# A four-part scheme for the first FFN layer extended to one more chunk of tokens, with attention visits, residual loads and operand splits moved earlier

## The chip, the cores and the metric

One core of one Trainium2 chip runs the whole kernel. The metric is the device time of one execution in microseconds (us); the time before is the median of three runs. Engines are called PE (TensorE; PEld its weight loads), DVE (VectorE), ACT (ScalarE), POOL (GpSimd) and SP (SyncE, which here issues most DMAs). Each engine runs its instructions in the order in which the code writes them.

## The reference

```
# attention, 8 batches x 8 heads, 576 tokens, head size 64
mask  = band of 32 (heads 0-3)  or  every 32nd earlier token (heads 4-7)
attn  = softmax(where(mask, q @ k.T / 8, -1e9)) @ v
x     = attn, heads side by side          # [8, 576, 512]
# layer norm and feed-forward
xn    = (x - mean(x)) / sqrt(var(x) + 1e-6) * g_ln
out   = x + relu(xn @ w_ch1) @ w_ch2      # w_ch1 [512, 2048], w_ch2 [2048, 512]
```

## The kernel before

**Tiles and chunks.** The 8 x 576 token rows are cut into nine chunks of 512: chunk c < 8 holds the first 512 tokens of batch c, chunk 8 the last 64 tokens of all batches. In the code `wide` is 7, `FIRST` is 3, A is chunk 7 and Z is chunk 8. The hidden size 2048 is 16 blocks f of 128. All matmuls of the feed-forward run on pairs of float32r tiles, a high part and a rest ("hi", "lo", made by `split_x`: ACT copies the high part, DVE or POOL subtracts), three matmuls for one product. The mean and the scale of the layer norm are folded into the weights and into a factor per row that is applied at the end (`x_scale` makes it from a load of x, `finish` applies it).

**Stages.** Chunk 0 is interleaved with the first attention by a word list (`ORDER`). Chunks 1 and 2 are `plain`: for each f, twelve matmuls of 512 columns of the first layer (`ffn1`), relu, and twelve of the second layer (`group`). Chunks 3 to 5 run `pair(c, p)` eight times, for two blocks f each: seven products of 128x256 blocks (`product2`, Strassen's scheme in Winograd's form: P1 a11 b11, P6 s2 t2, P5 s1 t1, P2 a12 b21, P7 s3 t3, P4 a22 t4, P3 s4 b22, in that order) in place of eight, sums on DVE (`add2`), and second-layer groups between the products. The operands b.. and t.. of x are staged in freed weight tiles (`stage_x`, `move`), sums t.. by POOL (`stage_sums`), then split (`x_split`). Sums of weights are made by POOL (`w_sums`), stored to DRAM (sd) and loaded again one pair ahead (`stage_w`, `split_w`). Chunk 6 is `plain` again. The joint part runs chunks 7 and 8 together in the same scheme with 512 columns, over operands `whole`/`halfs`, with weights that come back from DRAM through rings (`w_fetch`, `s_fetch`, `s_split`). Then the second layer of Z.

**Attention visits.** A batch has four head pairs. A visit does the scores of the next pair and the values of the present one on PE, then mask, division and maximum on DVE, subtraction on POOL, exp on ACT, a transpose on DVE, a store to DRAM and a load of the turned weights (pd, pt). In plain chunks the generator `pieces` hands out steps, four for each f; in `pair` a visit stands at every even p. Before the change, chunk c visits the four pairs of batch c + 1.

**Lines that the prediction touches.** L1214 `move` copies a weight half over one that `a_store` (L1243) has saved to DRAM (ad). L745/L747 load x for the residual and L752 (`x_scale`) reads it; in `half_c` the tables are

```
LOADS.update({2: (12, 13, 13, 14), **{u: (4, 5, 8, 9) for u in range(FIRST, wide - 1)}})
SCALES.update({2: (14, 15, 15, NFC), **{u: (7, 7, 11, 11) for u in range(FIRST, wide - 1)}})
```

L574 is the division of a visit, L1326 `add2`, L1148 `turn` (a DVE transpose of what `tail`, L773, loads for chunk 8), L721 and L802 the subtractions of splits, L867/L874 `ffn1`, L884 its rest part hl, L916 the second layer, L1321 `product2`, L1491 the joint products.

Of the kernel before, what the change touches and what calls it, by code (L numbers as in the profile page):

```python
# [63 lines left out]
def kernel(  # L64
# [10 lines left out]
    nc = tc.nc  # L75
# [257 lines left out]
    class Pair:  # L333
# [280 lines left out]
        def x_blocks(self, xT=None):  # L614

            cc = self.h0 // 2
            if xT is None and self.b == 2:
                xT = self.xo.rearrange("p t h d -> p (t h d)")[:, 0:CH]
            if xT is not None:
# [3 lines left out]
            elif self.b == B - 2:  # L623
                nc.vector.transpose(spread[cc], self.xraw.rearrange("p (i x) -> p i x", i=2))
            else:
                d, j = divmod(cc, 2)
                for i, name in enumerate((("b11", "t1"), ("b21", "b22"))[d]):
                    nc.vector.transpose(stage_x(name)[:, j], self.xraw[:, HC * i:HC * (i + 1)])
                if d == 0 and (self.b > 3 or j):
                    stage_sums(j)  # L630
# [174 lines left out]

# [27 lines left out]
    def whole_tile(i, names):  # L833
        t = wp.tile([P, 2, CH], F32, tag=f"w1_{i}", name=f"whole{i}_{names[0]}")
# [251 lines left out]
    def pieces(i0, i1):  # L1086
        for i in range(i0, i1):
            now = pairs[i] if i >= 2 * NHP else None
            nxt = pairs[i + 1] if i + 1 < NP else None
            short = i < 3 * NHP - 1 or i in (29, 30)  # L1090
            later = i in (3 * NHP, 3 * NHP + 1)
            soon = short and nxt and not nxt.local
            m_piece(now, nxt)
            yield
            if i + 2 < NP:
                pairs[i + 2].load_v()
# [3 lines left out]
            if now:  # L1100
                now.x_raw(nc.scalar)
            if nxt:
                nxt.p_turned()
            yield
            if nxt:
                nxt.v_sums()
# [22 lines left out]
            if later:  # L1129
                now.x_blocks()  # L1130
# [4 lines left out]
    gen = pieces(2 * NHP - 1, 4 * NHP)  # L1135
# [11 lines left out]
    def turn(cc):  # L1147
# [3 lines left out]
    last_steps = {  # L1151
        1: [lambda: tail(2)],
        3: [lambda: whole_tile(1, ("b220", "b120")), lambda: turn(2)],
        4: [lambda: tail(0)],
        5: [lambda: half_x(4, "b220")],
        6: [lambda: turn(0), lambda: whole_tile(2, ("t10", "t20")), lambda: whole_tile(3, ("t30", "t40")),
            lambda: sums_x(0, nc.gpsimd)],
        7: [lambda: half_x(5, "t10"), lambda: half_x(6, "t20"), lambda: tail(3)],
        8: [lambda: half_x(7, "t30")],
        9: [lambda: half_x(8, "t40"), lambda: whole_tile(1, ("b221", "b121")), lambda: turn(3)],  # L1160
        10: [lambda: half_x(9, "b221")],
        11: [lambda: tail(1), lambda: s_fetch(0)],
        12: [lambda: s_split(0)],
        13: [lambda: turn(1), lambda: whole_tile(2, ("t11", "t21")), lambda: whole_tile(3, ("t31", "t41")),
             lambda: sums_x(1, nc.vector)],
        14: [lambda: half_x(11, "t11"), lambda: half_x(12, "t21"), lambda: half_x(13, "t31"),
             lambda: half_x(14, "t41"), lambda: w_fetch(0)],
        15: [lambda: w_fetch(1), lambda: s_fetch(1)],
    }

    A_RING, S_RING = (0, NFC - 1, 1), (10, 2, 3)
# [435 lines left out]
```

## Time and profile before

| | |
|---|---|
| median of 3 runs | 923.51 us (922.21 to 923.74) |
| profiled execution | 921.0 us, span 919.2 us |
| granted TensorE clock, mean | 0.986 |
| PE busy | 875.8 us (95%), 7837 instructions |
| DVE busy | 534.9 us (58%) |
| POOL busy | 323.7 us (35%) |
| ACT busy | 264.7 us (29%) |
| DMA | 142.42 MB, mean 155 GB/s |

The busy time of an engine counts its instructions' time; PE's matmuls overlap each other, so the distance between the starts of two matmuls, not the duration of one, tells what a matmul costs. A row of the timeline has start, duration, engine, line, operation, tiles and shape, and in brackets the idle time before it and what ended that.

### The profile page before, as it was taken

To read this page: it belongs to the slowest core of one execution; us is meant where nothing else is said; L and a number is where in the kernel's file an instruction comes from. 1 tells how busy PE (TensorE), PEld (TensorE's weight loads), DVE (VectorE), ACT (ScalarE), POOL (GpSimd) and SP (SyncE) were. 2 spreads that over 40 slices of the span, in tenths; PEclk is the share of its full clock that TensorE was granted. 3 is DMA by queue.
4 is the path that set the end of the run, shared out by engine and by line. 5 is a ranking of instruction groups with operands and counts; after the bars stand their busy time and mean duration, and the time that the engine had idled before them with its cause. 6 is when DMAs were issued, how large, how long until landed. Compare 5 with 4: busy or idle time off the path is not lost.

```text
span 919.2 us, 20228 instructions
## 1 busy us (share of the span) xinstructions
PE 875.8 (95%) x7837; PEld 730.0 (79%) x7837; DVE 534.9 (58%) x1108; ACT 264.7 (29%) x531; POOL 323.7 (35%) x380
## 2 busy tenths in 40 slices
PE   7799999999989979999999989999988999999997
PEld 6688888888878868888888878887766888787886
DVE  5899974556524457666756676666355442333443
ACT  3786631111111132233333242322112122111121
POOL 5787750011237834435534462331012111121000
PEclk9999999999999999999999999999999999999999
DMA  9899865577469786979796969777663252331111
GB/s 188 196 287 249 254 122 112 125 158 145 88 173 205 197 191 163 216 182 195 179 199 160 225 146 217 166 213 159 152 114 94 48 184 92 116 102 46 41 52 47
DMA packets 381545, 142.42 MB, mean 155 GB/s; under 512 B 297605, under 2 KB 361993, under 8 KB 381449
## 3 DMA queue, kind: packets, MB, share of 16 engines
q1 hardware_dynamic: 298120, 126.24, 55.2%
q10 hardware_dynamic: 83328, 14.89, 9.4%
q8 instruction: 62, 1.02, 0.5%
q14 instruction: 35, 0.28, 0.1%
HBM read 100.37 MB, written 40.70 MB: 153 GB/s over the span
## 4 chain that ended last, share of the span: by engine, by line
PE 31%; DMA 9%; DVE 5%; SPq 3%; issue 1%; ACT 1%; ACTq 0%; POOL 0%; DVEq 0%; POOLq 0%
PE po L916 16%; PE x L1491 7%; PE x L1321 4%; DMA pd<-sm 2%; PE ph L867 1%; DMA v_l<-in_v_dram 1%; DMA pt<-pd 1%; SPq L773 1%; DMA x<-xds 1%; PE m L455 1%; DVE hz L1510 1%; DVE u L1326 1%; PE ph L874 1%; PE n L524 1%; DMA v_s<-in_v_dram 1%
## 5 line engine op out<-in xcount | busy, mean ns | idle before, releaser
L916 PE MATMUL po<-w,hh 128*128 128x512 f32 x768 | 241.2, 396 | 0.0
L916 PEld LDWEIGHTS po<-w,hh 128*128 128x128 f32 x768 | 143.3, 190 | 29.9 <-issue 0.4
L916 PE MATMUL po<-w,hq 128*128 128x512 f32 x576 | 160.2, 394 | 0.9 <-DVE x L890 0.7
L916 PE MATMUL po<-w,hl 128*128 128x512 f32 x384 | 150.6, 392 | 0.0
L916 PEld LDWEIGHTS po<-w,hq 128*128 128x128 f32 x576 | 97.4, 189 | 12.5 <-ACT w L1257 0.8
L884 DVE SCALAR_TENSOR_TENSOR hl<-ph,hh 128x512 fp32r<-128x512 f32 x64 | 43.8, 684 | 97.2 <-ACT hh L879 97.2
L501 POOL TENSOR_TENSOR sm<-sm,mx 128x640 f32<-128x640 f32 (+1 forms) x31 | 40.2, 1298 | 139.2 <-DVE mx L496 125.8
L1321 PE MATMUL x<-xh_b,w 128*128 128x256 f32 x384 | 84.3, 282 | 2.7 <-DVE p L1326 1.6
L916 PEld LDWEIGHTS po<-w,hl 128*128 128x128 f32 x384 | 72.7, 189 | 15.6
L879 ACT ACTIVATE hh<-ph 128x512 fp32r<-128x512 f32 x64 | 38.0, 593 | 145.0 <-PE ph L874 121.4
L867 PE MATMUL ph<-xh,w 128*128 128x512 f32 x188 | 75.2, 400 | 2.4 <-DVE hl L884 2.4
L867 PE MATMUL ph<-xl,w 128*128 128x512 f32 x188 | 74.0, 394 | 0.0
L1258 POOL TENSOR_TENSOR w<-sw,w 128x256 fp32r<-128x256 f32 x48 | 37.6, 804 | 102.9 <-ACT w L1257 81.6
L1321 PEld LDWEIGHTS x<-xh_b,w 128*128 128x128 f32 x384 | 65.4, 188 | 10.0 <-issue 3.0
L757 POOL TENSOR_TENSOR rs<-rs,mhalf 128x1 f32<-128x1 f32 x36 | 20.2, 562 | 146.6 <-DVE rs L756 146.5
L1321 PE MATMUL x<-xl_b,w 128*128 128x256 f32 x192 | 53.8, 280 | 0.0
L507 ACT ACTIVATE sm<-sm 128x648 f32<-128x648 f32 (+1 forms) x32 | 23.8, 744 | 98.5 <-POOL sm L501 98.5
L874 PE MATMUL ph<-xh,w 128*128 128x512 f32 x188 | 51.2, 395 | 0.0
L1192 POOL TENSOR_TENSOR rings<-stage,rings 128x512 fp32r<-128x512 f32 x16 | 20.6, 1290 | 79.9 <-ACT rings L1191 79.9
L867 PEld LDWEIGHTS ph<-xh,w 128*128 128x128 f32 x188 | 35.5, 189 | 10.1 <-DVE hl L884 2.8
L874 PEld LDWEIGHTS ph<-xh,w 128*128 128x128 f32 x188 | 35.7, 191 | 7.6
L867 PEld LDWEIGHTS ph<-xl,w 128*128 128x128 f32 x188 | 35.6, 189 | 7.1
(232 smaller groups left out, 1683.8 us busy)
## 6 DMA issues: line engine op xcount, KB each, us to landing
s<-in_moe_w_ch_dram SPq DMA_DIRECT2D x32, 512.0 KB
sw<-sd SPq DMA_DIRECT2D x48, 256.0 KB
out_dram<-x SPq DMA_DIRECT2D x32, 256.0 KB
raw<-in_q_dram SPq DMA_DIRECT2D x108, 72.0 KB
raw<-in_k_dram SPq DMA_DIRECT2D x108, 72.0 KB
wd<-w SPq DMA_DIRECT2D x24, 256.0 KB
ringa<-wd SPq DMA_DIRECT2D x24, 256.0 KB
xds<-xo SPq DMA_DIRECT2D x32, 162.0 KB
```

Source lines behind the costliest of these rows:

```text
L501: eng.tensor_tensor(out=sm, in0=sm, in1=mx[:, :, 0:nt].unsqueeze(3).broadcast_to([P, 2, nt, sm.shape[3]]), op=ALU.subtract)
L507: nc.scalar.activation(out=self.smv, in_=self.smv, func=AF.Exp, scale=SCALE)
L757: nc.gpsimd.tensor_tensor(out=rs, in0=rs, in1=mhalf, op=ALU.pow)
L867: nc.tensor.matmul(ph, w1h[:, cc], x[:, cc, :], start=(new and n == 0 and i == 0), stop=False)
L874: nc.tensor.matmul(ph, w1l[:, cc], xt[c][0][:, cc, :], start=False, stop=(cc == NCC - 1))
L879: nc.scalar.activation(out=hh, in_=ph, func=AF.Relu)
L884: nc.vector.scalar_tensor_tensor(out=hl, in0=ph, scalar=0.0, in1=hh.bitcast(F32), op0=ALU.max, op1=ALU.subtract)
L916: nc.tensor.matmul(po[c, i], hx, w, start=(n_po[c, i] == 0 and n == 0), stop=(n_po[c, i] == NFC - 1 and n == 2))
L1192: nc.gpsimd.tensor_tensor(out=t[:, :, 1], in0=stage[n], in1=t[:, :, 0].bitcast(F32), op=ALU.subtract)
L1258: nc.gpsimd.tensor_tensor(out=w[:, 1], in0=t[:, k], in1=w[:, 0].bitcast(F32), op=ALU.subtract)
L1321: nc.tensor.matmul(ps, wx, xx[:, j], start=(start and j == 0 and i == 0), stop=(j == 1 and i == 2), skip_group_check=not start)
L1491: nc.tensor.matmul(ps, wx, xx, start=(start and j == 0 and i == 0), stop=(j == 1 and i == 2), skip_group_check=not start)
```

## The change

Chunk 6 runs `pair` like chunks 3 to 5. Every visit stands one place earlier: chunk 1 and 2 do ten visits in place of nine, chunk c's visit at p = 0 is already the second pair of batch c + 1, and chunk 6 has three visits. The first pair of a batch is visited at p = 6 of the chunk before, its x comes back from DRAM at p = 1 and is staged at p = 3. In the last pair of chunks 3 to 5 each operand is split right behind the product that used it last (`X_AT`); in the last Strassen chunk a table (`final`) places the loads, turns, sums and splits for the joint part. The stores and reloads of saved weight halves (ad, `a_store`, `a_back`, `back`) go. Six of the eight `w_sums` move from chunk 2 to chunk 1. Residual loads of chunk 2 go to steps 4, 5, 7, 8 and the scales to 7, 8, 10, 11; in pairs there is one load for each of p = 2 to 5 and one scale at the end of p = 3 to 6. The joint part begins with pairs 7 and 6, whose weights are still in SBUF, has rings of 3 and 2 tiles where there were 3 and 3, one spare tile where there were two, and the product s1 t1 two places later.

```
-    SUMS_AT = 1, 2, 5, 6, 7, 9, 10, 11
-    plain(1, NT)
+    plain(1, {f: [partial(w_sums, p)] for p, f in enumerate((1, 2, 3, 9, 11, 13))}, NT)
...
+    plain(2, {
+        1: [partial(w_sums, 6)],
+        2: [partial(w_sums, 7)],
+        3: [pairs[3 * NHP].x_blocks],
+        7: [pairs[3 * NHP + 1].x_blocks],
+        11: [partial(stage_sums, 0)],
+        12: [partial(stage_sums, 1), partial(stage_w, 0)],
+        13: [partial(x_split, "b11")],
+        14: [partial(x_split, "t2"), partial(x_split, "t1"), partial(split_w, 0), partial(stage_w, 1)],
+        15: [partial(stage_w, 2)],
+    }, 1)
...
+    final = {
+        (1, "P1"): [lambda: whole_tile(1, ("b210", "b110"))],
+        (1, "P6"): [lambda: tail(2)],
+        (2, "P6"): [lambda: tail(0)],
+        (2, "P3"): [lambda: whole_tile(5, ("b220", "b120")), lambda: turn(2)],
+        (3, "P1"): [lambda: whole_tile(0, ("b211", "b111"))],
+        (3, "P5"): [lambda: turn(0)],
+        (3, "P2"): [lambda: half_x(3, "b220", G)],
+        (3, "P7"): [lambda: tail(3), lambda: whole_tile(11, ("t10", "t20")),
+                    lambda: whole_tile(2, ("t30", "t40")), lambda: sums_x(0, G)],
...
+        (4, "P4"): [lambda: tail(1)],
+        (4, "P3"): [lambda: whole_tile(5, ("b221", "b121")), lambda: turn(3)],
...
+        (5, "P4"): [lambda: turn(1)],
...
+    X_AT = dict(P1="b11", P6="t2", P5="t1", P2="b21", P7="t3", P4="t4", P3="b22")
...
+        i = NHP * (c + 1) + 1 + p // 2
+        now, nxt, soon, far = (pairs[k] if k < NP else None for k in range(i, i + 4))
+        off = 2 + fin
...
+        if 0 <= p - off < NT:
+            res[c].append([x_load(c, p - off)])
...
+        if 0 <= p - off - 1 < NT:
+            k = p - off - 1
+            res[c][k].append(x_scale(res[c][k][0], f"{c}_{k}"))
...
-    for c in range(FIRST, wide - 1):
+    for c in range(FIRST, wide):
         for p in range(NFC // 2):
-            if c == wide - 2 and p == 6:
-                back(0)
-                for n in (1, 3, 4):
-                    a_back(n)
             pair(c, p)
     late_low()
-    run_groups(len(groups))
-    for p in (6, 7):
-        a_back(p)
-    gen = pieces(NP - NHP, NP)
-    plain(wide - 1, NT)
```

What stands in three rows of instructions. First SP's queue where the first two weight sums are stored (f are the sums, sd and ad DRAM buffers, raw the loads of q and k, xdl and xds the stores of attention's output), before, in chunk 2:

```order
L363 DMA raw3_1_3309<-in_k_dram 32x18x32 x4
L827 DMA sd_204<-f0_0_3318 128x2x256
L829 DMA sd_204<-f1_0_3320 128x256 x2
L1243 DMA ad_205<-w1_1_856 256x1x256
L827 DMA sd_204<-f0_1_3363 128x2x256
L829 DMA sd_204<-f1_1_3365 128x256 x2
L1243 DMA ad_205<-w1_3_1033 256x1x256
```

and the same sums after, in chunk 1:

```order
L362 DMA raw2_3_2248<-in_k_dram 32x18x32 x4
L827 DMA sd_204<-f0_0_2257 128x2x256
L829 DMA sd_204<-f1_0_2259 128x256 x2
L827 DMA sd_204<-f0_1_2299 128x2x256
L829 DMA sd_204<-f1_1_2301 128x256 x2
L591 DMA xds_202<-xo_195 54x6x128 x2
```

The stores to ad are gone and the rest stands a chunk earlier. Next DVE at the end of chunk 2 and the first visit of chunk 3 (x2_.. are loads of x, n and m the PSUM tiles of the visit, xl_a and xl_b rest parts of the operands), before:

```order
L802 TENSOR_TENSOR xl_a_3159<-staged5_3656,xh_a_3158 128x512 x2
L884 SCALAR_TENSOR_TENSOR hl2_15_4198<-ph2_15_4183,hh2_15_4196 128x512
L752 BN_STATS st2_1_4205<-x2_1_4115 128x6
L754 BN_AGGR mv2_1_4207<-st2_1_4205 128x2
L756 TENSOR_SCALAR rs2_1_4209<-mv2_1_4207 128x1
L752 BN_STATS st2_2_4212<-x2_2_4118 128x6
L754 BN_AGGR mv2_2_4214<-st2_2_4212 128x2
L756 TENSOR_SCALAR rs2_2_4216<-mv2_2_4214 128x1
L802 TENSOR_TENSOR xl_b_4220<-staged11_3920,xh_b_4219 128x512
L574 TENSOR_TENSOR xo_195<-n16_4230,den0_197 128x5x64
```

and after:

```order
L798 TENSOR_TENSOR xl_a_3304<-staged5_3805,xh_a_3303 128x512
L887 SCALAR_TENSOR_TENSOR hl2_15_4311<-ph2_15_4296,hh2_15_4309 128x512
L482 TENSOR_TENSOR sm0_191<-m17_4325,mask_s_137 128x2x5x54
L482 TENSOR_TENSOR sm0_191<-n17_4326,mask_s_137 64x54
L482 TENSOR_TENSOR sm0_191<-m17_4325,mask_s_137 64x54
L573 TENSOR_TENSOR xo_195<-n17_4326,den1_198 128x4x64
```

No reader of a load of x stands between the last hl and the visit any more. Last, DVE from the last products of p = 5 to the visit of p = 6 in chunk 3 (u2, u3 the sums, x4 and x3 PSUM tiles of products), before:

```order
L1326 TENSOR_TENSOR u3_2144<-x4_3_5_5172,u3_2144 128x256
L1337 SCALAR_TENSOR_TENSOR hq3_11_2_5158<-p1_2142,hq3_11_2_5158 128x256
L752 BN_STATS st3_2_5185<-x3_2_4994 128x6
L754 BN_AGGR mv3_2_5187<-st3_2_5185 128x2
L756 TENSOR_SCALAR rs3_2_5189<-mv3_2_5187 128x1
L752 BN_STATS st3_3_5192<-x3_3_5064 128x6
L754 BN_AGGR mv3_3_5194<-st3_3_5192 128x2
L756 TENSOR_SCALAR rs3_3_5196<-mv3_3_5194 128x1
L1326 TENSOR_TENSOR u2_2143<-x3_3_5_5122,u2_2143 128x256
L1337 SCALAR_TENSOR_TENSOR hq3_11_0_5180<-u3_2144,hq3_11_0_5180 128x256
```

and after:

```order
L1274 TENSOR_TENSOR u3_2143<-x4_3_5_5276,u3_2143 128x256
L1285 SCALAR_TENSOR_TENSOR hq3_11_2_5262<-p1_2141,hq3_11_2_5262 128x256
L1274 TENSOR_TENSOR u2_2142<-x3_3_5_5221,u2_2142 128x256
L1285 SCALAR_TENSOR_TENSOR hq3_11_0_5284<-u3_2143,hq3_11_0_5284 128x256
L748 BN_STATS st3_2_5302<-x3_2_5084 128x6
L750 BN_AGGR mv3_2_5304<-st3_2_5302 128x2
L752 TENSOR_SCALAR rs3_2_5306<-mv3_2_5304 128x1
```

The sum u2, which empties the PSUM tile x3, stands ahead of the scale now, and one scale where there were two.

## Rows read from the trace of the kernel before

**Rows 1.** Stages: length, busy us and count per engine, clock, DMA share, GB/s.
```profile
core 0: us, PE busy (x) PEld busy (x) DVE busy (x) ACT busy (x) POOL busy (x), PEclk, DMA share, GB/s
238.03:337.93 99.90, 97.08 (x956) 79.21 (x954) 46.13 (x93) 17.76 (x31) 56.97 (x63) 0.98 0.73 175
337.93:630.73 292.80, 278.14 (x2854) 244.26 (x2855) 196.70 (x475) 91.37 (x241) 124.16 (x150) 0.99 0.80 187
630.73:744.13 113.40, 104.22 (x821) 82.86 (x820) 56.62 (x113) 21.91 (x40) 15.27 (x14) 0.95 0.48 110
744.13:866.40 122.27, 121.07 (x525) 97.56 (x524) 44.05 (x72) 22.51 (x39) 21.41 (x19) 1.00 0.29 94
```

**Rows 2.** Who PE waited for: us in total, times, longest.
```profile
PE ph L867 <- DVE hl L884: 8.3, 6, 2.5
PE m L455 <- DVE u L1326: 5.3, 8, 1.0
PE x L1321 <- DVE xo L574: 5.0, 1, 5.0
PE n L524 <- DMA pt<-pd: 3.2, 2, 3.0
PE x L1321 <- DVE p L1326: 1.6, 2, 0.8
PE x L1321 <- DVE hq L1337: 1.0, 2, 0.7
```

**Rows 3.** Stretches right behind four of these waits, columns as in Rows 1.
```profile
271.90:277.30 5.40, 5.40 (x17) 4.29 (x18) 2.59 (x10) 1.35 (x2) 3.31 (x3) 0.68 0.31 83
344.40:348.00 3.60, 3.37 (x13) 3.11 (x14) 3.48 (x12) 0.00 (x0) 3.60 (x3) 0.53 0.21 56
682.20:685.60 3.40, 3.37 (x8) 2.69 (x9) 0.70 (x1) 0.00 (x0) 0.00 (x0) 0.52 0.39 108
710.60:716.50 5.90, 5.90 (x83) 4.76 (x84) 2.61 (x9) 0.00 (x0) 0.55 (x1) 0.50 0.18 54
```

**Rows 4.** Timeline of chunk 2 around 270 us, ACT and PE.
```profile
269.80 0.63 ACT L1214 ACTIVATE w<-w 128x512 fp32r<-128x512 f32 x1 [9.80 <-DMA ad<-w]
271.86 0.50 PE L867 MATMUL ph<-xh,w 128*128 128x512 f32 x1 [2.38 <-DVE hl L884]
```

**Rows 5.** Timeline at the entry to chunk 3, DVE and PE.
```profile
340.44 0.69 DVE L752 BATCH_NORM_STATS2 st<-x 128x6 f32<-128x512 f32 x1 [2.56 <-DMA x<-xds]
342.24 0.69 DVE L752 BATCH_NORM_STATS2 st<-x 128x6 f32<-128x512 f32 x1 [0.71 <-DMA x<-xds]
344.63 0.55 PE L1321 MATMUL x<-xh_a 128*128 128x256 f32 x1 [5.02 <-DVE xo L574]
```

**Rows 6.** Timeline of chunk 6, SP, DVE and PE.
```profile
659.27 6.02 SPq L773 DMA_DIRECT2D xt<-xds  x8
667.19 0.71 DVE L1148 STREAM_TRANSPOSE whole_b<-xt 128x512 f32<-128x512 f32 x1 [6.78 <-DMA xt<-xds]
682.23 0.72 PE L867 MATMUL ph<-xh_b,w 128*128 128x512 f32 x1 [2.46 <-DVE hl L884]
```

**Rows 7.** Timeline of PE: starts of two pairs, then of two plain blocks.
```profile
392.91 0.39 PE L1321 MATMUL x<-xh_a,w 128*128 128x256 f32 x1
403.51 0.28 PE L1321 MATMUL x<-xh_a,w 128*128 128x256 f32 x1
...
733.25 0.39 PE L867 MATMUL ph<-xh_b,w 128*128 128x512 f32 x1
738.69 0.39 PE L867 MATMUL ph<-xh_b,w 128*128 128x512 f32 x1
```

**Rows 8.** Timeline of DVE: one split's subtraction, beside POOL work and without.
```profile
334.39 1.06 DVE L802 TENSOR_TENSOR xl_a<-staged,xh_a 128x512 fp32r<-128x512 f32 x1 [0.97 <-ACT xh_a L801]
...
343.27 0.69 DVE L802 TENSOR_TENSOR xl_b<-staged,xh_b 128x512 fp32r<-128x512 f32 x1
```

**Rows 9.** Part 5 of the page: one split's subtraction on POOL.
```profile
L1192 POOL TENSOR_TENSOR rings<-stage,rings 128x512 fp32r<-128x512 f32 x16 | 20.6, 1290 | 79.9 <-ACT rings L1191 79.9
```

More of the change, by code (lines that the diff above doesn't have):

```diff
@@ L1150 @@
     tails = {}
[L1151 to L1171, printed above, removed]
+    A_RING, S_RING = (15, 12, 13), (1, 0)
+    SEQ = [NFC // 2 - 1, NFC // 2 - 2, *range(NFC // 2 - 2)]
     stage, ring = {}, {}
@@ L1262, in plain @@
+    n_end = NFC * (wide - FIRST)
+    def plain(c, events, n_groups):
         for f in range(NFC):
[L1263 to L1265 removed]
             ph = ffn1(c, f)
@@ L1346, in late_low, with tail, turn, hidden @@
             late.pop().low()
+    def tail(cc):
+        tails[cc] = tail_raw(cc)
+    def turn(cc):
+        nc.vector.transpose(whole[f"b{cc // 2 + 1}2{cc % 2}"], tails.pop(cc))
+    h_z = []
+    def hidden():
+        att_ctx.close()
+        hb = ctx.enter_context(tc.tile_pool(name="hb", bufs=1))
+        h_z.extend(hb.tile([P, CH], F32, name=f"hz{f}") for f in range(NFC))
+        for k in range(4):
+            whole[f"t{k + 1}1"] = h_z[8 + k]
+    def in_a(k):
+        return tuple(t[:, k] for t in xa_t)
@@ L1381, in pair @@
         add2(u2_t, x2, p1_t)
-        if even:
-            pairs[i + 2].load_v()
-        else:
-            now.x_blocks()
-        half_c(c, 2 * p)
-        if last and more:
-            x_split("b11")
+        turns = soon.t_pieces() if soon and not even else iter(())
+        next(turns, None)
+        if even and soon:
+            soon.load_v()
+        if 0 <= p - off < NT:
+            res[c].append([x_load(c, p - off)])
+        events("P6")
         run_groups(1)
@@ L1391, in pair @@
         product2(p, "s1", "t1", x3)
-        turn = pairs[i + 2].t_pieces() if not even else iter(())
-        next(turn, None)
+        next(turns, None)
+        events("P5")
         run_groups(1)
@@ L1397, in pair @@
         q.low()
-        next(turn, None)
-        if even:
+        split_w(n + 2)
+        if even and nxt:
             nxt.p_turned()
-        if n + 2 < n_end:
-            split_w(n + 2)
-        if even:
-            now.x_raw(nc.scalar, range(2))
-        if last and more:
-            x_split("t2")
-            x_split("t1")
+        elif now and not even and not last:
+            now.x_blocks()
+            if p > 1 and not fin:
+                stage_sums(p // 2 - 1)
+        events("P2")
         run_groups(1)
@@ L1412, in pair @@
         q22 = Quarter(c, 2 * p + 1, 2, p1_t)
-        if even:
-            now.x_raw(nc.scalar, range(2, 4))
-        elif i + 3 < NP:
-            pairs[i + 3].load_qk()
-        if last:
-            late_x(c, 0)
+        if even and now and p < NFC // 2 - 2:
+            now.x_raw(nc.scalar, range(2))
+        elif not even and far:
+            far.load_qk()
+        events("P7")
         run_groups(1)
@@ L1424, in pair @@
         q22.low()
-        if n + 4 < n_end:
-            stage_w(n + 4)
-        if even:
-            nxt.v_sums()
-        half_c(c, 2 * p + 1)
-        if last:
-            late_x(c, 1)
+        stage_w(n + 4)
+        if even and now and p < NFC // 2 - 2:
+            now.x_raw(nc.scalar, range(2, 4))
+        if p == 1:
+            pairs[NHP * (c + 1)].x_raw(nc.sync)
+        events("P4")
         run_groups(1)
@@ L1487, in product @@
+    def product(pos, name, x, ps, start=True):
+        w = weight(pos, name)
         for j in range(2):
```

344 lines of the change are left out of this document (161 added, 183 removed).

## The prediction

> **What bounds the kernel now.** I read the stage windows first: in every stage PE is busy nearly all the time, 97.1 of 99.9 us in chunk 2, 278.1 of 292.8 in chunks 3 to 5, 104.2 of 113.4 in chunk 6, 121.1 of 122.3 in the joint part [rows 1]. DVE has 197 of 293 and POOL 124 of 293 in the Strassen chunks. So the time is PE's products, its idle gaps, and the stretches in which its clock stands at half. A change can pay only by fewer PE columns, a gap that goes, or a stretch that returns from the 1.2 GHz level (0.5 in the clock column) to the 2.4 GHz level (1.00).
>
> Next the list of who PE waits for [rows 2]: hl 8.3 us, u 5.3, xo 5.0, pt 3.2, and p and hq 2.6 together. Then the windows right behind the four longest waits: 0.68, 0.53, 0.52 and 0.50 of full clock for 3.4 to 5.9 us [rows 3], while the stages stand at 0.95 to 1.00 as a whole. A wait of 2.4 to 5 us of PE is thus paid twice: once idle, once with the matmuls behind it slowed. I price each as wait + length × (1 − clock). Last, the timeline at each wait says what came late.
>
> The sum is made against the profiled execution, 921.0 us; the median of the timed runs, 923.5, is 2.5 above it, and I add that at the end.
>
> **PE's work.** Chunk 6 becomes eight Strassen pairs. A pair without a visit takes 403.51 − 392.91 = 10.60 us, two plain blocks 2 × 5.44 = 10.88 [rows 7]: 8 × 0.28 = 2.2 us less. That is small because the seven products pay in matmuls of 256 columns and their sums and splits go to DVE, ACT and POOL. The count of visits stays the same, one only moves from chunk 6 to chunk 2, so their work cancels. Bounds: 0 (if the pairs of chunk 6 run like those with short waits) to 2.2; I take 2.2, since the row is of the same code.
>
> **Chunk 2's stall.** An ACT copy of w at the head of its queue waits 9.80 us for the ad store to leave the same buffer, the high part of h stands behind it in that queue, DVE's hl behind that, and PE waits 2.38 [rows 4]. The ad stores are gone, the buffer is read by engines alone. Removed: 2.4 + 5.40 × 0.32 = 4.1. What replaces the reader: the sums are made from SBUF while it is resident, by POOL, which has 57 of 99.9 us in this chunk [rows 1] and gives up six of its eight weight sums to chunk 1. Bounds 0 to 4.1; I take 4.1, as nothing on ACT waits for a DMA there any more.
>
> **Entry to chunk 3.** DVE stands at two scales whose loads of x came late (2.56 and 0.71), the visit's division xo is queued behind them, and PE's first product waits 5.02 for xo [rows 5]. In the new order no scale stands between the last hl of chunk 2 and the visit, and the loads, scales and splits of the first operands stand some blocks of 5.4 us earlier. Removed at most 5.0 + 3.60 × 0.47 = 6.7. Late next: the operand t4, split on ACT and POOL in the first pair; ACT's half and POOL's subtraction of 1.29 [rows 9] start behind the visit's own ACT work. I leave 0.8 for that, so 5.9; bounds 3 (a wait of 2.4 with its clock stays) to 6.7.
>
> **Chunk 6.** Two kinds of wait are there. hl: the turn (the transpose of xt) stands at the head of DVE's queue and waits 6.78 us for the tail's DMA issued at 659.27, and hl behind it comes late; of the 8.3 us of hl waits 5.9 lie here (all but chunk 2's 2.4), with a slow stretch of 3.40 × 0.48 = 1.6 [rows 2, 3, 6]. pt: one visit waits 3.0 for its load, and 5.90 × 0.50 = 2.95 follows [rows 2, 3]. Both are removed in this form: there is no hl in chunk 6 any more (a pair closes on sums in PSUM), and each visit's pd and pt traffic is issued one place earlier. At most 5.9 + 1.6 + 3.0 + 2.95 = 13.5. New waits of the kind that the Strassen chunks have: two of about 0.4 behind u and p, and perhaps one turn that is late by about 1 us. The turns still stand in DVE's queue, four of them, but the tails are issued a pair and more ahead (over 10.6 us), and the one shown took 7.9 from issue to use (659.27 to 667.19). I take 13.5 − 2 = 11.5; bounds 0 (every turn as late as before) to 13.5.
>
> **The small waits of chunks 3 to 5.** u 5.3 in eight waits, p 1.6, hq 1.0: 7.9 in all [rows 2]. The u waits come where the scales of the next chunk stand ahead of the sum that empties the PSUM tile which the visit then uses. In the new order the sum stands first and one scale instead of two follows; x's splits are spread operand by operand over the last pair. Bounds 0 to 7.9, and I take 5.5: the u waits gone, most of the p and hq waits left, since one operand more is split beside the last products. DVE's sum of busy time (196.7 of 292.8) leaves room for it.
>
> **Joint part.** It starts with pairs 7 and 6, already resident, so no load stands ahead of its first products; but PE idles only 122.27 − 121.07 = 1.2 us there [rows 1]. Bounds 0 to 1.2; 0.6. The ring of two tiles for the sums is as short as before, but one sum (ACT and POOL's 1.29 [rows 9]) is less than a position's products.
>
> **Sum.** 2.2 + 4.1 + 5.9 + 11.5 + 5.5 + 0.6 = 29.8; 921.0 − 29.8 = 891.2; with 2.5 added 893.7. With the profile's own offset uncertain by 1 or 2 us I say 893. All upper bounds together give 35.6, or 888; half of the taken chunk-6 and small-wait terms lost gives 902. The forecast's own range is 887 to 901.
>
> **Rivals.**
> *Late turns.* DVE gets Strassen's sums and splits in chunk 6 and is in order: a turn that waits as in [rows 6] now holds up u, p and hq, which PE's tiles wait for. A turn that is 5 us late costs PE that and 1.6 of clock, 6.6. Two of four late: +13, 907. For it: that chunk before had exactly this wait. Against it: the distance of more than a pair.
>
> *Half of the stalls move.* The chain from x's load to scale, split and first product is shifted, not shortened; loads and visits' transfers share queues, and DMA is at 0.73 to 0.80 in chunks 2 to 5 [rows 1]. If each stall comes back at half its size: 893.7 + 15 = 909. Against it: DMA is at 0.48 in chunk 6, where the largest term lies.
>
> *DVE held by POOL.* In chunk 6 some 11 DVE instructions with two operands in SBUF (seven splits, four sums) now run beside POOL's. A split beside POOL work took 1.06 us against 0.69 [rows 8]: 11 × 0.37 = 4.1 us of DVE time, which lies beside PE's 85 us of pairs and costs nothing by the sum. If each had to stand out a whole POOL instruction of 1.29 [rows 9] and PE waited for it: 11 × 1.29 = 14.2, 908. Against it: the row shows a stretch of 0.37, not of 1.29. The Trainium skill ("SBUF — State Buffer", section "Who interferes with whom") says that a DVE instruction with both inputs in SBUF and a GpSimd instruction that reads SBUF share a port pair, that the one issued first holds it for its whole length and the other stands still. By that rule the rival's 908 holds; the row of 1.06 agrees with a wait for the rest of a POOL instruction only, and no row here shows a DVE split held for a whole one.
>
> *Slower.* The ten visits of chunks 1 and 2 come every three blocks (3 × 5.44 = 16.3 us), and six weight sums on POOL, with their stores on SP, move into chunk 1, ahead of a visit's own stores in both queues. A visit whose pt is late costs 3.0 + 2.95 = 6.0, as the one in chunk 6 [rows 2, 3]. From the sixth late one (36 > 29.8) the kernel is slower; with eight of ten late it is 893.7 + 48 = 942. For it: POOL is busy 57 of 100 us in chunk 2 and DMA 0.73 of the time. Against it: chunk 2 has a single long wait and that for ACT.
>
> **Chances.** Forecast 0.58, late turns 0.16, half of the stalls 0.10, DVE held 0.07, slower 0.09. A measurement of this kernel can tell about 0.2% (1.8 us) from no change. The first four are all faster, save for the edge of the half case where it becomes a whole one (0.03 to no change, with a little of the slower case): faster 0.88, same 0.03, slower 0.09. Up to 909 lie the forecast, the late turns, DVE's case and about half of the third; below 884 nothing is left by the bounds, so 884 to 910.
>
> **What will show it.** Right: no wait of ACT for a DMA of w in chunk 2 and a clock of 1.00 there; no 5 us wait at the entry to chunk 3; pairs of 10.6 us in chunk 6 and a stage clock near 1.00; waits of m for u below 2 us in all. Wrong: turns in DVE's queue that wait over 3 us for xt with PE waiting for u or p behind them (late turns); waits of PE for xo or pt in chunks 1 and 2 (slower); waits of the same names at other places, summing to 12 us or more (half); splits of 2 us on DVE (held).

## The result and the profile after

The changed kernel took 898.1 us (median of four runs, 895.9 to 902.3) against 922.9 before: ratio 0.974, 95% interval 0.969 to 0.978. Beside the variants below it took 899.6, and there the ratio was 0.978 (0.974 to 0.981). The profiled execution took 895.9 with a span of 894.1, so 25.1 us less than the profiled one before; the forecast sum was 29.8.

Stage windows first, cut so that the products in each are the same in both kernels (columns as in [rows 1]). Before, chunk 1, chunks 3 to 5, chunk 6 and the joint part:

```profile
142.04:238.03 95.99, 95.99 (x894) 78.85 (x893) 53.43 (x110) 15.84 (x25) 8.56 (x9) 1.00 0.66 134
...
337.93:631.93 294.00, 279.34 (x2860) 245.24 (x2861) 197.83 (x478) 91.42 (x242) 124.16 (x150) 0.99 0.80 187
631.93:744.13 112.20, 103.02 (x815) 81.88 (x814) 55.49 (x111) 21.86 (x39) 15.27 (x14) 0.95 0.48 109
744.13:864.80 120.67, 119.47 (x517) 96.24 (x516) 42.76 (x70) 22.51 (x39) 21.41 (x19) 1.00 0.29 95
```

After, the same stages with chunk 2 (which answers to the first row of [rows 1], 99.90) in second place:

```profile
142.62:242.62 100.00, 98.12 (x1010) 80.37 (x1009) 56.75 (x119) 15.86 (x25) 42.21 (x46) 1.00 0.72 161
242.62:340.78 98.16, 95.35 (x956) 78.05 (x954) 52.33 (x109) 18.72 (x32) 29.09 (x33) 1.00 0.71 154
340.78:629.83 289.05, 282.06 (x2863) 242.59 (x2860) 200.03 (x476) 96.31 (x250) 134.72 (x159) 1.00 0.77 179
629.83:720.65 90.82, 90.28 (x833) 79.72 (x833) 62.16 (x139) 34.28 (x87) 44.69 (x47) 1.00 0.52 125
720.65:839.65 119.00, 119.00 (x526) 98.57 (x525) 44.20 (x74) 22.46 (x39) 20.82 (x19) 1.00 0.26 87
```

Two things are moved between stages and are taken out here. One is a visit of 1.8 us (a pair with a visit behind it takes 12.4 us from start to start, one without 10.6). It goes from chunk 6 to chunk 1, which has 1010 matmuls for 894; the prediction has it in chunk 2, whose 956 stay. The other is nine matmuls of 0.227 us of the second layer, which go from chunk 6 to the joint part. What is left, gain positive:

| stage | measured gain, us | forecast |
|---|---|---|
| before chunk 1 | -0.6 | 0 |
| chunk 1 | 95.99 + 1.8 - 100.00 = -2.2 | 0 |
| chunk 2 | 1.7 | 4.1 |
| entry and chunks 3 to 5 | 294.00 - 289.05 = 5.0 | 5.9 + 5.5 |
| chunk 6 | 112.20 - 90.82 - 1.8 - 2.0 = 17.6 | 2.2 + 11.5 |
| joint part | 120.67 - 119.00 + 2.0 = 3.7 | 0.6 |

The clock of every stage is 1.00 now (0.98 and 0.95 before in chunks 2 and 6). Who PE waited for, in the same form as [rows 2]:

```profile
PE n L523 <- DMA pt<-pd: 3.2, 3, 1.3
PE x L1269 <- DVE hq L1285: 3.1, 6, 0.8
...
PE po L919 <- DVE x L893: 1.5, 1, 1.5
...
PE x L1269 <- DVE u L1274: 1.2, 2, 1.0
...
PE x L1269 <- ACT p L1379: 1.0, 1, 1.0
```

The waits for hl, for xo at the entry and of m for u are gone. The sum for pt (a visit's turned weights) reads 3.2 in both kernels, and it is not the same wait: before, one of 3.0 in chunk 6; now three of about 1 us in chunks 1 and 2, where there was none. The wait for x at 252 us is new as well.

### The profile page after: what moved, and what is told of

Same layout as the page of the kernel before. It is cut to its first block, busy times and chain, and to the rows that moved or that the text cites. A ratio compares the mean times of both kernels' runs of the same rounds, so it can differ in the third digit from the quotient of the medians.

```text
span 894.1 us, 20778 instructions
## 1 busy us (share of the span) xinstructions
PE 866.9 (97%) x7981; PEld 729.1 (82%) x7981; DVE 554.8 (62%) x1162; ACT 283.5 (32%) x588; POOL 368.2 (41%) x427
## 4 chain that ended last, share of the span: by engine, by line
PE 73%; DMA 10%; DVE 5%; SPq 3%; POOL 3%; issue 2%; ACT 1%; ACTq 1%; DVEq 0%; POOLq 0%
PE po L919 34%; PE x L1269 14%; PE x L1487 9%; PE ph L870 7%; PE ph L877 3%; DMA pd<-sm 2%; PE m L454 2%; DMA pt<-pd 2%; PE n L523 1%; DMA sw<-sd 1%; SPq L362 1%; POOL f L826 1%; PE m L523 1%; DVE kt_s L428 1%; DMA xo<-xds 1%
## 5 line engine op out<-in xcount | busy, mean ns | idle before, releaser
L919 PE MATMUL po<-w,hq 128*128 128x512 f32 x768 | 213.6, 394 | 0.0
L919 PE MATMUL po<-w,hh 128*128 128x512 f32 x640 | 199.7, 393 | 1.6 <-DVE x L893 1.5
L919 PEld LDWEIGHTS po<-w,hq 128*128 128x128 f32 x768 | 129.8, 189 | 14.1
L919 PEld LDWEIGHTS po<-w,hh 128*128 128x128 f32 x640 | 118.0, 188 | 26.5 <-ACT hh L882 1.9
L919 PE MATMUL po<-w,hl 128*128 128x512 f32 x320 | 124.8, 390 | 0.0
L1269 PE MATMUL x<-xh_b,w 128*128 128x256 f32 x512 | 113.5, 285 | 6.5 <-DVE hq L1285 3.1
L1269 PEld LDWEIGHTS x<-xh_b,w 128*128 128x128 f32 x512 | 87.3, 188 | 19.2 <-DVE hq L1285 7.2
L1215 POOL TENSOR_TENSOR w<-sw,w 128x256 fp32r<-128x256 f32 x64 | 52.4, 839 | 100.7 <-ACT w L1214 89.6
L500 POOL TENSOR_TENSOR sm<-sm,mx 128x640 f32<-128x640 f32 (+1 forms) x31 | 40.6, 1309 | 90.4 <-DVE mx L495 67.1
L1269 PEld LDWEIGHTS x<-xl_b,w 128*128 128x128 f32 x256 | 48.1, 188 | 5.0 <-POOL xl_b L798 0.5
L1164 POOL TENSOR_TENSOR rings<-stage,rings 128x512 fp32r<-128x512 f32 x14 | 18.1, 1292 | 74.4 <-ACT rings L1163 74.4
L1282 ACT ACTIVATE hq<-u 128x256 fp32r<-128x256 f32 x64 | 26.8, 418 | 63.6 <-PE po L919 18.8
L1215 POOL TENSOR_TENSOR xh_a<-sw,xh_a 128x256 fp32r<-128x256 f32 x32 | 24.2, 755 | 50.8 <-ACT xh_a L1214 48.1
```

Source lines behind the costliest of these rows:

```text
L500: eng.tensor_tensor(out=sm, in0=sm, in1=mx[:, :, 0:nt].unsqueeze(3).broadcast_to([P, 2, nt, sm.shape[3]]), op=ALU.subtract)
L919: nc.tensor.matmul(po[c, i], hx, w, start=(n_po[c, i] == 0 and n == 0), stop=(n_po[c, i] == NFC - 1 and n == 2))
L1215: nc.gpsimd.tensor_tensor(out=w[:, 1], in0=t[:, k], in1=w[:, 0].bitcast(F32), op=ALU.subtract)
L1269: nc.tensor.matmul(ps, wx, xx[:, j], start=(start and j == 0 and i == 0), stop=(j == 1 and i == 2), skip_group_check=not start)
L1282: nc.scalar.activation(out=self.h[0], in_=src, func=AF.Relu)
```

## The experiments

All variants start from the changed kernel. Stage lengths are read at the same points of every trace, in us; the median is of up to six runs, the ratio is to the kernel before on the same chip.

| run | chunk 1 | chunk 2 | chunks 3 to 5 | chunk 6 | joint | median | ratio (95%) |
|---|---|---|---|---|---|---|---|
| changed kernel | 100.5 | 100.8 | 288.3 | 91.0 | 119.0 | 899.6 | 0.974 to 0.981 |
| sums in chunk 2 | 98.2 | 112.1 | 286.9 | 92.6 | 119.0 | 910.3 | 0.985 to 0.991 |
| division first | 99.8 | 98.9 | 282.7 | 90.3 | 119.0 | 893.7 | 0.967 to 0.974 |
| x back by SP | 99.6 | 99.2 | 290.9 | 90.3 | 119.0 | 896.2 | 0.971 to 0.977 |
| joint order of before | 102.7 | 100.7 | 288.0 | 91.0 | 123.2 | 905.0 | 0.980 to 0.986 |
| scale first | 102.6 | 100.7 | 292.8 | 90.9 | 119.0 | 900.8 | 0.975 to 0.982 |
| late tails | 101.5 | 100.5 | 288.6 | 98.0 | 119.0 | 906.0 | 0.981 to 0.987 |
| ad stores | 99.8 | 110.9 | 285.9 | 91.0 | 119.0 | 908.3 | 0.985 to 0.991 |
| SP order | 101.4 | 97.8 | 282.7 | 90.4 | 119.0 | 892.5 | 0.967 to 0.972 |
| finish first | 103.3 | 96.9 | 283.7 | 90.3 | 119.0 | 890.5 | 0.965 to 0.970 |
| x back later | 100.8 | 96.4 | 281.5 | 91.4 | 119.0 | 889.2 | 0.963 to 0.968 |

### The changed kernel once more

> The changed kernel once more, beside its variants on the same chip. Theory (the time is set by PE's products and by small waits that the trace of the changed kernel names): 894 to 902 us, ratio to before 0.970 to 0.978, with the same waits of PE: n for pt 3.2 us in three visits of chunks 1 and 2, x for hq and u about 4 us. Rival (the gain is partly a matter of DMA timing, different in each execution): the median leaves 894 to 902, or the waits for pt and the wait for x at 250 us are gone in this profile.

899.6 us (898.0 to 903.2), with the same waits; the three for pt came to 4.8 us. The longest was 2.5 in place of 1.3, and the clock behind it stood at 0.64 for 4.7 us. So two executions of one program differ by 3.2 us in chunks 1 and 2 together. An effect below that is read from the stage that it belongs to.

### Weight sums back in chunk 2

```
-    plain(1, {f: [partial(w_sums, p)] for p, f in enumerate((1, 2, 3, 9, 11, 13))}, NT)
+    plain(1, {}, NT)
...
+        1: [partial(w_sums, 0)], 2: [partial(w_sums, 1)], 5: [partial(w_sums, 2)], 6: [partial(w_sums, 3)],
+        7: [partial(w_sums, 4), ...], 9: [partial(w_sums, 5)], 10: [partial(w_sums, 6)], 11: [partial(w_sums, 7), ...]
```

> The changed kernel with all eight weight sums in chunk 2, at the places of the kernel before (f = 1, 2, 5, 6, 7, 9, 10, 11). Theory A (the stores of the sums to sd on SP's queue stand ahead of the stores pd<-sm and make the visits at 181 and 219 us wait for pt): the waits for pt of 0.8 and 1.1 us there go, -1.9 to -2.4 us, and as much or less comes back at visits of chunk 2 where the stores now stand; total -3 to +2 us against the changed kernel. Rival B (pt is late because each visit's loads are issued a place earlier and DMA is full): the waits at 181 and 219 us stay, the time is unchanged within 1 us. Under both, no 5 us stall as in chunk 2 of the kernel before, since nothing is stored to ad.

The waits at 181 and 219 us are gone, as A said. The total was missed by both: 10.7 us slower, with PE waiting 7.1 us for hl once, and a clock of 0.50 behind that, though nothing is stored to ad. (1.6 of the 10.7 lie in chunk 6, which the edit does not touch.) ACT in this variant, then POOL and DVE:

```profile
338.46 0.74 ACT L506 ACTIVATE sm<-sm 128x640 f32<-128x640 f32 x1 [14.75 <-POOL sm L500]
339.11 0.58 ACT L882 ACTIVATE hh<-ph 128x512 fp32r<-128x512 f32 x1
...
337.18 1.26 POOL L500 TENSOR_TENSOR sm<-sm,mx 128x640 f32<-128x640 f32 x1
...
339.72 0.69 DVE L887 SCALAR_TENSOR_TENSOR hl<-ph,hh 128x512 fp32r<-128x512 f32 x1 [11.94 <-ACT hh L882]
```

The last sums and the sums of x stand ahead of the softmax subtraction on POOL; ACT's exponent waits for that, the high part of h stands behind it, then hl, then PE. The early sums are thus worth more than the waits that they cause.

### The division ahead of the masks

```
+            now.v_divide(av[0:2])
             if nxt:
+                if not nxt.local:
+                    parts[0:2] = parts[1], parts[0]
                 nxt.s_mask(parts)
-            now.v_divide(av)
+            now.v_divide(av[2:])
```

> The changed kernel with one edit in the pairs: a visit's division of the rows in the PSUM tile n comes ahead of the masking of the next scores, as in the kernel before. Theory A (the second product of each pair with a visit waits for the tile n, which the division empties too late; it makes these pairs 10.9 us where they were 10.6): these pairs return to 10.6, 12 pairs in chunks 3 to 5 and 2 to 3 in chunk 6, -3.5 to -4.5 us. Rival B (the wait is for ACT's copy p or another engine's operand): the pairs stay at 10.9 and the time moves less than 1 us. Rival C (the masking now ends later, so the exponent, pd and pt come later): the pairs return to 10.6 but waits for pt of 0.5 us or more appear, net 0 or slower.

In the kernel before, a visit's first division stood ahead of the masks of the next scores; in the changed kernel it stands behind them. The list of changes ahead of the prediction does not name this. A holds: chunks 3 to 5 are 5.6 us shorter than in the run beside it. They take 285.9 to 289.1 us in the six executions that have the changed kernel's code in these chunks, and 282.7, 282.7 and 283.7 in the first three that have the division first. The starts of one pair with a visit before it and of the next, in the changed kernel and then in the variant:

```profile
392.06 0.39 PE L1269 MATMUL x<-xh_a,w 128*128 128x256 f32 x1
...
402.94 0.28 PE L1269 MATMUL x<-xh_a,w 128*128 128x256 f32 x1
```

```profile
388.71 0.39 PE L1269 MATMUL x<-xh_a,w 128*128 128x256 f32 x1
...
399.31 0.28 PE L1269 MATMUL x<-xh_a,w 128*128 128x256 f32 x1
```

10.88 against 10.60, as it was before ([rows 7], which show a pair with a visit ahead of it too). DVE says why, changed kernel and variant (the visit's scores and averages end at the same point of the pair):

```profile
392.20 0.72 DVE L482 TENSOR_TENSOR sm<-m,mask_s 128x540 f32<-128x540 f32 x1 [1.38 <-PE m L523]
...
393.08 0.54 DVE L573 TENSOR_TENSOR xo<-n,den 128x256 f32<-128x256 f32 x2
```

```profile
388.80 0.55 DVE L573 TENSOR_TENSOR xo<-n,den 128x256 f32<-128x256 f32 x2 [1.34 <-PE m L523]
389.27 0.20 DVE L482 TENSOR_TENSOR sm<-n,mask_s 64x54 f32<-64x54 f32 x1
```

The second product goes into the buffer of n and waits until the division has read it, 0.9 us later here. Eleven such pairs in chunks 3 to 5 lose 11 x 0.3 = 3.3 us, each piece too short for the list of waits; the twelfth, the first of chunk 3, takes 11.5 us either way. The other 2.3 us of the gain lie in the pairs at p = 3, shorter in this execution; why is not shown.

### x loaded back by SP

```
-            now.x_raw(nc.scalar, range(2))
+            now.x_raw(nc.sync, range(2))
```

(and the same for the other two loads).

> The changed kernel with the four loads of a visit's x back from DRAM issued by SP in place of ACT. Theory A (these loads, at the head of ACT's queue, wait for the store before them and hold up the high parts hq behind them, which makes PE wait 3.2 us at 380 to 386 and 2.0 at 480 to 484): those waits go, -4 to -6 us. Rival B (SP's queue takes over the wait: weight loads and pd stores behind it come later): new waits of PE for sw's split or pt, net -1 to +6 us.

Inconclusive. In the profile B's picture: PE waits 6.8 us for p (4.0 once) where it had waited for what stood behind ACT's loads, and chunks 3 to 5 are 2.6 longer. The median is 3.4 lower, and the runs (894.6 to 901.9) overlap those of the changed kernel.

### The joint part in the order of before

```
+        product(k, "s1", "t1", x3)
         product(k, "a12", "b21", x1, False)
...
-        product(k, "s1", "t1", x3)
         add(h_z[2 * p + 1], x3, u3)
```

(and the second-layer work that stood behind the product s3 t3 moves ahead of it).

> The changed kernel with the order of products of the kernel before in the joint part: s1 with t1 ahead of a12 with b21, so that only a product's length lies between the sums u3 and hz and the next product into the same PSUM tile. Theory A (in the kernel before each of the eight positions lost 0.46 us there, a wait of 0.15 for hz and slower matmuls behind it, and the order took that away): positions of 15.4 us where the changed kernel has 15.0, +3 to +4 us. Rival B (the joint part gained because it begins with resident pairs, and has fewer loads beside it): positions stay at 15.0, within 1 us.

A: 123.16 against 119.00 in this stage; the other 1.2 us of the median's 5.4 lie outside, where chunk 1 is 2.2 longer in this execution. The matmuls that wait, in this variant and then in the changed kernel:

```profile
L1487 PE MATMUL x<-half_b,rings 128*128 128x512 f32 x42 | 11.6, 411 | 1.0 <-DVE hz L1512 0.2
```

```profile
L1487 PE MATMUL x<-half_b,rings 128*128 128x512 f32 x42 | 10.7, 389 | 0.0
```

The idle time that the list shows is 1.0 us; the loss is four times that. It sits in two matmuls of each position, as one of them shows in this variant:

```profile
753.34 1.07 PE L1487 MATMUL x<-half_t,w 128*128 128x512 f32 x4
754.56 0.96 PE L1487 MATMUL x<-half_b,rings 128*128 128x512 f32 x3
```

The last of the four starts at 754.02, the next matmul 0.54 us later and the one after it 0.34, where 0.23 is the rule. That is 0.43 us in seven of the eight positions, and 0.95 in the first. The kernel before has 0.54 and 0.34 in all eight, the changed kernel in none.

### The scale ahead of the sum u2

```
+        if 0 <= p - off - 1 < NT:
+            ...x_scale...
         add2(u2_t, x3, u2_t)
```

(and the same lines go from behind the sum).

> The changed kernel with the scale of x (statistics, then one small instruction) ahead of the sum u2 in the last slot of a pair, as in the kernel before. Theory A (a scale there makes the sum late, and the visit, whose scores go into the PSUM tile that the sum reads, waits): waits of m for u of 0.4 to 1.0 us at the visits of p = 4 and 6 in four chunks, +3 to +6 us. Rival B (with the masks and divisions in the new order the visit's tile isn't the one that decides): less than +1 us.

B by the waits: no wait of m for u came back, and the median rose by 1.2, within what single executions differ by. (The 292.8 of the table is of the slowest of six executions, 906.3 us, with waits for p and xh_a at p = 3.) So the eight waits of before did not hang on the order alone. In the kernel before two scales stood ahead of that sum and v_sums of the visit in the slot before; with one, the sum is still in time. Two were not tried, so what removed these waits stays open.

### Late tails

```
-        (1, "P6"): [lambda: tail(2)],
+        (2, "P4"): [lambda: tail(2)],
```

(and the other three alike, one slot ahead of their turn; in the changed kernel the code has them 7 to 12 slots ahead).

> The changed kernel with the four tails of chunk 6 loaded one slot (1.4 us) ahead of their turn in place of 9 to 14 slots. Theory A (the distance between a tail and its turn is what keeps DVE's queue free; a turn at its head waits for the whole transfer of some 8 us): each turn waits 5 to 7 us and PE 3 to 6 us behind each, with a slower clock after it: +14 to +26 us. Rival B (a pair's tiles give PE enough ahead that DVE's wait is mostly covered): +1 to +8 us.

Chunk 6 is 7.0 us longer: B's upper end. Two of the four turns wait for their loads at the head of DVE's queue, 6.19 and 1.77 us, and only the first reaches PE (4.2 us for u, and a clock of 0.50 behind it). That one turn makes nearly all of the loss, 4.2 + 5.0 x 0.50 = 6.7:

```profile
675.97 0.71 DVE L1300 STREAM_TRANSPOSE whole_b<-xt 128x512 f32<-128x512 f32 x1 [6.19 <-DMA xt<-xds]
681.84 0.71 DVE L1300 STREAM_TRANSPOSE whole_b<-xt 128x512 f32<-128x512 f32 x1 [1.77 <-DMA xt<-xdl]
...
680.00:685.00 5.00, 4.78 (x17) 4.10 (x18) 2.84 (x8) 0.42 (x1) 2.29 (x2) 0.50 0.27 69
```

### The ad stores put back

```
+    def a_store(p):
+        nc.sync.dma_start(ad[p], low1[p].bitcast(F32))
...
+        1: [..., partial(a_store, 0)], 2: [..., partial(a_store, 1)], 5: [partial(a_store, 2)], ...
```

> The changed kernel with the eight stores to ad put back in chunk 2, at the places of the kernel before (f = 1, 2, 5, 6, 7, 9, 10, 11), the weight sums staying in chunk 1. Nothing reads ad. Theory A (ACT's copy of w waits for the store that still reads the same buffer; that alone made the wait of 2.4 us in chunk 2): ACT waits for ad<-w again for 3 us or more at one of the three copies, PE 1 to 5 us behind it, +2 to +8 us. Rival B (it was the weight sums on POOL in chunk 2, as the variant with the sums there shows 8.4 us of waits for hl with no store to ad at all): no wait for ad of more than 1 us on ACT, time within 1.5 us.

A, beyond its upper end: 8.7 us slower, chunk 2 10.1 longer. ACT and PE of this variant:

```profile
272.78 0.63 ACT L1187 ACTIVATE w<-w 128x512 fp32r<-128x512 f32 x1 [7.04 <-DMA ad<-w]
302.88 0.63 ACT L1187 ACTIVATE w<-w 128x512 fp32r<-128x512 f32 x1 [8.23 <-DMA ad<-w]
303.01 0.34 ACTq L647 DMA_DIRECT2D pt<-pd  x1
...
PE n L524 <- DMA pt<-pd: 9.0, 3, 7.2
PE ph L871 <- DVE hl L888: 3.1, 1, 3.1
```

The chain of [rows 4] is back, with 7.0 in place of 9.8 on ACT and 3.1 in place of 2.4 on PE; a second copy, 8.2 us late, holds up the load of pt in ACT's queue, and PE's wait of 7.2 for it is the larger part of the loss.

### Three repairs on top of the division first

The three runs add one edit each.

```
-    plain(1, {f: [partial(w_sums, p)] for p, f in enumerate((1, 2, 3, 9, 11, 13))}, NT)
+    plain(1, {f: [partial(w_sums, p)] for p, f in enumerate((1, 2, 4, 10, 11, 13))}, NT)
+    LOADS[2] = 4, 6, 7, 8
```

> The variant with the division first, and two weight sums of chunk 1 one block later (f = 4 and 10 for 3 and 9) and one load of x of chunk 2 one block later (f = 6 for 5). On SP's queue the stores pd<-sm then stand ahead of those sd stores and of that load, nothing else changes. Theory A (the visits at about 181, 219 and 295 us wait for pt since pd<-sm stands behind those in SP's queue): the three waits, 3.2 to 5.6 us together, fall below 1 us, and the time is 3 to 6 us below the variant with the division first alone (893.7): 888 to 891. Rival B (the transfer itself is slow beside the others, or pd<-sm waits for something else): the waits stay within 1 us of 3.7 and the time within 2 us.

SP's queue in the changed kernel, the stores to sd and the load of x ahead of pd<-sm, with DVE's and POOL's rows of the two tiles that are stored, and then SP in this variant:

```profile
169.56 2.75 SPq L407 DMA_DIRECT2D v_s<-in_v_dram  x6
174.06 0.39 SPq L827 DMA_DIRECT2D sd<-f  x1
174.49 0.96 SPq L829 DMA_DIRECT2D sd<-f  x2
175.57 1.88 SPq L637 DMA_DIRECT2D pd<-sm  x4
...
171.63 0.83 DVE L633 STREAM_TRANSPOSE sm<-sm 128x640 f32<-128x640 f32 x1
...
173.29 0.74 POOL L826 TENSOR_TENSOR f<-f 128x256 f32<-128x256 f32 x1
...
286.43 0.37 SPq L741 DMA_DIRECT2D x<-xdl  x1
287.31 0.56 SPq L743 DMA_DIRECT2D x<-xds  x1
288.59 1.82 SPq L637 DMA_DIRECT2D pd<-sm  x4
```

```profile
171.28 2.79 SPq L407 DMA_DIRECT2D v_s<-in_v_dram  x6
175.68 1.76 SPq L637 DMA_DIRECT2D pd<-sm  x4
```

In the changed kernel sm is ready at 172.46, and SP stands from 172.31 to 174.06 for POOL's sum f and stores that first. In this variant pd<-sm starts 31.2 us behind the start of chunk 1 (144.51) in place of 33.0 (142.62). For two of the three waits the cause is A's: the one at 181 us is gone and that at 295 is 0.3. The size is not: 892.5 against 893.7. At 219 us PE still waits 1.2, with the sd stores behind pd<-sm; the profile names a load of k on the same queue. That visit's wait goes when all sums leave chunk 1, so it hangs on them, but not on this order alone. PE also waits 1.3 for hl at 231 and 2.2 for x at 254: what the pt waits had hidden is next.

```
+            early = 2 if (c, f) == (2, 0) else 4
-            for _ in range(4):
+            for _ in range(early):
                 next(gen, None)
...
+            for _ in range(4 - early):
+                next(gen, None)
```

> As the variant before it, and in the first block of chunk 2 the four finishing instructions of chunk 1's rows stand ahead of the two transposes of q and k in DVE's queue. Theory A (PE's wait of 1.5 us for x at about 250 us is for these, held up by the transposes' 2.5 us): that wait falls below 0.3 us, -1 to -2 us. Rival B (the wait moves to the visit that needs the transposed q and k, or to hl): within 1 us.

The wait of 2.2 for x is gone and chunk 2 is 0.9 shorter, with 1.0 for hl in its place; the median fell by 2.0. Chunk 1, which the edit doesn't touch, is 1.9 longer in the profile. So the wait hung on the transposes, as A has it, and about half of it moved, as B has it; the intervals of the two runs overlap.

```
-        if even and now and p < NFC // 2 - 2:
-            now.x_raw(nc.scalar, range(2))
...
-            now.x_raw(nc.scalar, range(2, 4))
+            now.x_raw(nc.scalar, range(2))
...
+            now.x_raw(nc.scalar, range(2, 4))
         events("P3")
```

> As the variant before it, and the four loads of a visit's x back from DRAM are issued by ACT one slot later each, behind the high parts hq that stood behind them. Theory A (ACT's queue head waits for the store of x before them; the hq, p and splits behind it make PE wait about 3 to 5 us in all at p = 3 of the three Strassen chunks): waits of PE for hq, p, xh_a and u in chunks 3 to 5 fall from some 6 us to under 3, -2 to -4 us. Rival B (the x blocks now come later than the transposes that read them, and DVE stands at them): new waits of PE for u or p, 0 to +5 us.

What it moves is seen in ACT of the changed kernel: the issues of xo<-xds at the head of the queue, and the high parts hq behind them.

```profile
376.51 1.10 ACTq L603 DMA_DIRECT2D xo<-xds  x2
377.72 0.42 ACT L1282 ACTIVATE hq<-u 128x256 fp32r<-128x256 f32 x1 [4.17 <-DMA v_s<-in_v_dram]
378.00 2.63 ACTq L603 DMA_DIRECT2D xo<-xds  x2
380.76 0.42 ACT L1282 ACTIVATE hq<-u 128x256 fp32r<-128x256 f32 x1 [2.62 <-DMA x<-xds]
```

What these issues themselves wait for, the store of x or another transfer, is not shown: the rows name loads of v and of x.

A in part: at p = 3 one wait of 0.4 is left in the three chunks, and the three pairs there take 38.2 us together (42.3 before the edit, 40.8 to 48.1 in the nine other runs in which ACT issues them where the changed kernel does). New waits come at p = 1, 0.7 and less in these chunks, where the three pairs are 2.0 longer together, and 1.4 for hq at 644 us in chunk 6. Chunks 3 to 5 are 281.5 (283.7 before the edit). The median of 889.2 us is not clear of the 890.5 before the edit; with a ratio of 0.966 (0.963 to 0.968) the version with all repairs beats both kernels.

## Why the prediction was right, and where its steps failed

The direction, the size (898 in the own range of 887 to 901) and the place of the largest term were right. Five terms of the sum were mis-sized. That the total came so close is partly luck: against the table, the forecast was 11.6 us too high in chunks 1 to 5 and ahead of them, and 7.0 too low in chunk 6 and the joint part.

- **PE's work, 2.2.** Right: the pairs of chunk 6 without a visit take 10.5 to 10.6 us. Those with a visit ahead take 10.9, by the order of masks and division.
- **Chunk 2's stall, 4.1.** The mechanism is shown: without ad stores ACT waits for no transfer of w, and with them back the wait returns. The step's bound named one cause, and that was not enough: the sums had to leave the chunk as well (the variant with them there lost 7.1 us at one place). Of the 4.1, 1.7 was left: a wait of 1.5 for x and one of 1.3 for pt are new in this chunk.
- **Entry and small waits, 5.9 + 5.5.** The step that failed most, and by what it put at nothing. What was to go went: no wait at the entry, none of m for u. From start to start, the first pair of chunk 3 takes 11.5 us (340.78 to 352.31) where it took 18.1 (337.93 to 356.03), 6.6 less; the pairs at p = 1, 5 and 7 are 6.6 shorter together. Both are more than forecast. Against them stand two losses that the sum does not have: 3.1 by the new order of masks and division in the other eleven pairs with a visit ahead, and 5.1 in the three pairs at p = 3 (44.2 us for 39.1). Of these the list shows three waits at 381 to 387 us, 2.7 together, and two at 481 to 484, 1.7. Where ACT issues its loads of x has much to do with them: one slot later again, the three pairs take 38.2 (with 2.0 of the gain lost at p = 1). Measured 5.0; 11.3 with the division first (282.7) and 12.5 with all repairs (281.5). No variant puts the late scales back at the entry, so its 6.6 is read from the wait that went.
- **Chunk 6, 11.5.** Too small: 17.6 - 2.2 = 15.4, more than the upper bound of 13.5. The bound summed the listed waits and the slow stretches. Of the latter it has all: in that chunk the clock stood below 1.00 only around the waits at 682 and 711 us. What it left out are pieces that no list shows. Blocks without a visit that start at 641.92 and 647.60 took 5.68 and 5.62 us without a wait, where an undisturbed one takes 5.44. Priced from the stage (112.2 less 16 blocks of 5.44, the visits and the nine matmuls) the bound would have been some 16. The new waits were near the 2 us allowed. No run here puts plain blocks back, so how the gain divides between the scheme and the earlier visits is read from the waits that went, not shown by a variant.
- **Joint part, 0.6.** The bound of 1.2 from busy time was wrong: a matmul that starts late still counts as busy. The sum also gave nothing for the later place of s1 t1, and that is what paid: 3.7 measured, 4.2 in the opposite experiment.

The rivals. *Late turns* had the right mechanism and a distance that excluded it: all four turns of the changed kernel waited 0.3 us or less. Its price for one was about right: the turn that waited 6.19 us cost some 6.7, against 6.6 for 5 us. What it had too high is how many turns come late and reach PE: with all four loads one slot ahead it was one. *DVE held* did not occur; the splits of chunk 6 on DVE read:

```profile
684.23 1.21 DVE L717 TENSOR_TENSOR half_t<-whole_t,half_t 128x512 fp32r<-128x512 f32 x1 [0.71 <-ACT half_t L716]
687.89 0.69 DVE L717 TENSOR_TENSOR half_t<-whole_t,half_t 128x512 fp32r<-128x512 f32 x1 [1.66 <-ACT half_t L716]
```

1.21 is the longest of seven, 0.5 over the shortest. The Trainium skill ("SBUF — State Buffer", "Who interferes with whom") has a DVE instruction with two SBUF inputs stand still while a GpSimd instruction that reads SBUF holds the shared port pair; the rows agree with a part of such an instruction, none with a whole one. *Slower* did happen, by its own sign (waits for pt in chunks 1 and 2), at a part of its price of 6.0: of the ten visits three came late, two of them by the sd stores and a load ahead of pd<-sm in SP's queue. In the profiled execution each cost 0.8 to 1.3 us and no clock; in the second one the longest cost 2.5 and 4.7 x 0.36 = 1.7 of clock. The Trainium skill ("Perfetto Trace Analysis", "What 'DMA-bound' means") names the issuing engine's sequencer as a bound of its own where its track is solid with DMA slices, and large descriptors as what helps. Here SP's queue is not solid, it stood 1.75 us for a sum, and putting the urgent store first was enough for two of the three waits. *Half of the stalls move* is the nearest: waits of the names in [rows 2] (pt, hq, u, p) come to 8.7 us in the profiled execution and 10.3 in the second one, where they were 24.4. That is below the 12 set as its sign, and the slow clock did not come back with them in the first.

## What to carry to other kernels

After a large reordering, ask of each buffer that two operations share who empties it now: a swap of two DVE instructions cost 3.3 us in pieces of 0.3 that no list of waits shows, and only lengths of equal pieces of work (10.88 against 10.60) gave it away. Price a stage from its length less its products, not from the listed waits, and never bound a loss by idle time alone. On a queue that works in order, whatever an engine waits for goes in ahead of what nobody needs yet.

## What the runs showed of the hardware that was not expected

The length of a wait alone does not say whether PE's clock falls behind it. Behind a wait of 3.0 us for hl the finish-first variant stood at 1.00, behind one of 2.0 us for pt the variant with the joint order of before stood at 0.57, and behind 7.2 us for pt the variant with ad stores at 0.51 (the 1.2 GHz level):

```profile
231.60:236.00 4.40, 4.15 (x18) 3.44 (x19) 4.14 (x8) 0.60 (x1) 4.09 (x6) 1.00 1.13 180
```

```profile
222.20:226.00 3.80, 3.77 (x78) 3.04 (x79) 2.62 (x10) 0.00 (x0) 1.43 (x3) 0.57 0.83 205
```

```profile
307.30:312.00 4.70, 4.53 (x80) 3.69 (x81) 3.13 (x10) 0.00 (x0) 0.85 (x1) 0.51 0.02 6
```

So pricing every wait of 2.4 us and more with a slow stretch, as the prediction does, holds for the waits that it was read from and not for all. What tells them apart stays open.
